# Residual scaling x + alpha·fx: a contiguous head for the first 30.5 KiB of each partition

## The chip, the cores and the metric

The kernel runs on one core of a Trainium2 chip. The metric is the device time of one execution in microseconds. All numbers of the profile come from one profiled execution; where nothing else is said, a time is counted from the start of that execution's span.

## The reference

The inputs `x` and `fx` have the shape 512 x 32 x 640 in bf16, 20.97 MB each, and `alpha` holds one bf16 number. The output has the shape of `x`:

```python
def reference(x, fx, alpha):
    return x + alpha * fx
```

Each byte of `x` and `fx` is read once, each byte of the output is written once: 62.9 MB in all.

## The kernel before

Each tensor is taken as one long row of numbers and cut into 128 equal parts, one for each partition: partition p owns the 160 KiB from p times 160 KiB on. The code counts in units of `K = 512` numbers, which is 1 KiB a partition in bf16 (128 KiB over all partitions), so that a partition's part has `ROW = 160` units. One tile `t` of 160 + 47.5 units holds everything. x lies at its own units 0 to 160, and the result is written over it. fx is put wherever the tile is free at that time, first over the later units of x that have not been loaded yet, then in the units 160 to 207.5.

The order of all work is written out by hand in `PLAN`, one step a line, and is the order in which the instructions stand on their engines:

- `x a b` loads units a to b of x (`load_x`, L96), `f a b p` loads units a to b of fx to place p of the tile (`load_f`, L100). Both are DMAs issued by SyncE (SP).
- `a` loads alpha (L104), spreads it over the partitions with one small matmul (L108) and copies it to `a_f` (L110).
- `m a b` multiplies units a to b of fx in place by alpha (L113), `c a b` adds them to x (L116). Both run on VectorE (DVE).
- `s a b` stores units a to b (L119), again from SP. A step behind a `|` names another step that this one has to wait for: the first store waits for the multiply of units 112.5 to 134.5.

Waits follow from the places in the tile. `x 95 160` writes over the place of fx 0 to 65 and so waits for the add over those units; `f 112.5 142.5 160` and `f 142.5 160 190` write over the place of fx 65 to 112.5 and wait for its adds. All DMAs are issued by SP in the order of the plan, on one queue (q1), so that a DMA whose wait is not over holds back those behind it. Each runs on 16 DMA engines, 8 partitions on each; each engine carries the same bytes. A row of a partition that is longer than 64 KiB is moved as two packets, any other as one. At the end SP waits for all but the last store (L131), and the program ends when the last store has landed.

The partition's part is named here:

```python
xv, fv, ov = (
    t.flatten_outer_dims().rearrange("(p n) d -> p (n d)", p=P) for t in (x, fx, out)
)
```

and `of(v, a, b)` (L87) cuts units a to b out of it, for loads and stores alike.

Of the kernel before, what the change touches and what calls it, by code (L numbers as in the profile page):

```python
# [1 line left out]

# [4 lines left out]

ALU = mybir.AluOpType
F32 = mybir.dt.float32

P = 128
K = 512
ROW = 160
SPARE = 47.5

LANES = 8

PLAN = """
f 0 8 95
a
f 8 65 103  # L30
x 0 64
x 64 95
f 65 112.5 160
m 0 8
m 8 65
c 0 8
c 8 64
c 64 65
x 95 160
m 65 95  # L40
c 65 95
f 112.5 142.5 160
m 95 112.5
c 95 112.5
f 142.5 160 190
m 112.5 134.5
s 0 64 | m 112.5 134.5
m 134.5 142.5
c 112.5 142.5
m 142.5 160  # L50
c 142.5 160
s 64 128
s 128 160
"""


@with_exitstack
def kernel(
    ctx: ExitStack,
    tc: tile.TileContext,  # L60
    x: bass.AP,
    fx: bass.AP,
    alpha: bass.AP,
    out: bass.AP,
):
    nc = tc.nc
    xv, fv, ov = (
        t.flatten_outer_dims().rearrange("(p n) d -> p (n d)", p=P) for t in (x, fx, out)
    )
    assert xv.shape[1] == ROW * K  # L70

    consts = ctx.enter_context(tc.tile_pool(name="consts", bufs=1))
    psum = ctx.enter_context(tc.tile_pool(name="psum", bufs=1, space=bass.MemoryType.PSUM))
    flat = ctx.enter_context(tc.tile_pool(name="flat", bufs=1))
    ctx.enter_context(tc.manual_schedule())
    t = flat.tile([P, int((ROW + SPARE) * K)], x.dtype, name="t")
    info = mybir.DependencyInfo(mybir.DependencyClass.Sync, mybir.DependencyReason.DATA)

    lanes = {}
    lies = []  # L80
    done = []

    def at(a, b):
        return t[:, int(a * K) : int(b * K)]

    def of(v, a, b):
        return v[:, int(a * K) : int(b * K)]  # L87

    def place(a, b):
        for c, d, p in reversed(lies):  # L90
            if c <= a and b <= d:
                return at(p + a - c, p + b - c)
        raise ValueError(f"fx {a} to {b} lies nowhere in one piece")

    def load_x(a, b):
        done.append(nc.sync.dma_start(out=at(a, b), in_=of(xv, a, b)))  # L96

    def load_f(a, b, p):
        lies.append((a, b, p))
        done.append(nc.sync.dma_start(out=at(p, p + b - a), in_=of(fv, a, b)))  # L100

    def load_alpha():
        a_n = consts.tile([LANES, 1], alpha.dtype, name="a_n")
        done.append(nc.sync.dma_start(out=a_n[:], in_=alpha[None, :].to_broadcast([LANES, 1])))  # L104
        ones = consts.tile([1, P], alpha.dtype, name="ones")
        nc.vector.memset(ones[:], 1.0)  # L106
        a_ps = psum.tile([P, 1], F32, name="a_ps")
        done.append(nc.tensor.matmul(a_ps[:], ones[:], a_n[0:1, :], start=True, stop=True))  # L108
        lanes["a"] = consts.tile([P, 1], F32, name="a_f")
        nc.vector.tensor_copy(out=lanes["a"][:], in_=a_ps[:])  # L110

    def multiply(a, b):
        done.append(nc.vector.tensor_scalar_mul(place(a, b), place(a, b), lanes["a"][:]))  # L113

    def add(a, b):
        done.append(nc.vector.tensor_add(at(a, b), at(a, b), place(a, b)))  # L116

    def store(a, b):
        done.append(nc.sync.dma_start(out=of(ov, a, b), in_=at(a, b)))  # L119

    does = {"x": load_x, "f": load_f, "a": load_alpha, "m": multiply, "c": add, "s": store}
    begun = {}
    for step in filter(None, PLAN.split("\n")):
        step, *later = step.split(" | ")
        what, *numbers = step.split()
        does[what](*map(float, numbers))
        begun[step] = done[-1]
        for other in later:
            tc.add_manual_dep(done[-1].ins, begun[other].ins.name, info, reason="begins late")

    rest = nc.sync.nop(nofuse=True)  # L131
    for i in done[:-1]:
        tc.add_manual_dep(rest.ins, i.ins.name, info, reason="all but the last store")


# [1 line left out]
_INS = ['x', 'fx', 'alpha']  # L137
_OUTS = [((512, 32, 640), 'bfloat16')]


# [23 lines left out]
```

## Time and profile before

| | before |
|---|---|
| median of the runs | 151.1 us (3 runs, 151.07 to 151.1) |
| the profiled execution's own time | 151.11 us |
| its span | 149.3 us |
| DMA packets, bytes | 1728, 62.92 MB |
| HBM read, written | 41.94 MB, 20.97 MB |
| DVE busy | 66.5 us in 16 instructions |

The span lies inside the profiled execution's own time; 1.8 us are outside of it. The granted clock was 1.0 throughout. A packet is the piece of one partition's row that a DMA engine moves at a time; the trace has its start, its length and its bytes, but not its engine. 192 of the 1728 packets are smaller than 512 B: alpha's and those that count up semaphores.

### The profile page before, as it was taken

The numbers are of one execution on the slowest core, as the hardware profiler recorded it, in microseconds if no ns is written. First come the engines' busy times: TensorE is split into PE (matmuls) and PEld (weight loads), VectorE is DVE, ScalarE is ACT, GpSimd is POOL, SyncE is SP. The second block draws the span as 40 slices with busy tenths as digits, with TensorE's granted clock in tenths as the row PEclk, the third lists the DMA queues.
The fourth block names the chain that finished last, engine by engine and source line by source line (L and its number), as shares of the span: only waits on it lengthen the run. The fifth ranks groups of instructions, "written<-read, shape, count | busy, mean of one in ns | idle before, by whom it ended". The sixth has DMA issues, their size and how long they took to land.

```text
span 149.3 us, 84 instructions
## 1 busy us (share of the span) xinstructions
PE 0.2 (0%) x1; PEld 0.1 (0%) x1; DVE 66.5 (45%) x16; POOL 0.2 (0%) x4
## 2 busy tenths in 40 slices
PE   0000000000000000000000000000000000000000
PEld 0000000000000000000000000000000000000000
DVE  0300008920069999029997093599997000000000
POOL 0000000000000000000000000000000000000000
DMA  5969998969699999999999999899896969697993
GB/s 147 603 281 500 500 461 351 562 281 562 281 408 451 438 417 443 456 429 428 428 428 428 417 444 469 378 526 492 351 562 281 562 281 562 281 562 307 456 474 167
DMA packets 1728, 62.92 MB, mean 421 GB/s; under 512 B 192, under 2 KB 192, under 8 KB 192
## 3 DMA queue, kind: packets, MB, share of 16 engines
q1 hardware_dynamic: 1728, 62.92, 98.0%
HBM read 41.94 MB, written 20.97 MB: 421 GB/s over the span
## 4 chain that ended last, share of the span: by engine, by line
DMA 38%; DVE 33%; another core or an unknown queue 4%; SPq 1%; issue 0%; DVEq 0%
DMA t<-in_x_dram 27%; DVE t L116 26%; DMA t<-in_fx_dram 11%; DVE t L113 7%; SPq L100 0%; SPq L104 0%; DVEq L116 0%
## 5 line engine op out<-in xcount | busy, mean ns | idle before, releaser
L116 DVE TENSOR_TENSOR t<-t 128x15360 bf16<-128x15360 bf16 (+4 forms) x7 | 43.6, 6252 | 16.6 <-DMA t<-in_x_dram 16.5
L113 DVE TENSOR_SCALAR t<-t,a_f 128x4096 bf16<-128x4096 bf16 (+4 forms) x7 | 22.8, 3265 | 25.7 <-DMA t<-in_fx_dram 25.7
L110 DVE COPY a_f<-a_ps 128x1 f32<-128x1 f32 x1 | 0.2, 159 | 5.2 <-PE a_ps L108 5.2
L106 DVE MEMSET ones<- 1x128 bf16 x1 | 0.2, 165 | 0.8 <-PEq L148 0.8
L108 PE MATMUL a_ps<-a_n,ones 1*128 1x1 bf16 x1 | 0.2, 158 | 6.0 <-DMA a_n<-in_alpha_dram 6.0
L148 POOL MEMSET const-bfloat16-1.0<- 128x1 bf16 x1 | 0.1, 102 | 0.0
L148 POOL MEMSET const-uint8-127<- 128x1 uint8 x1 | 0.1, 102 | 0.0
L148 POOL MEMSET const-float32-1.0<- 128x1 f32 x1 | 0.1, 99 | 0.0
L108 PEld LDWEIGHTS <-ones 1*128 1x128 bf16 x1 | 0.1, 98 | 1.0 <-DVE ones L106 1.0
L148 POOL MEMSET const-float32-0.0<- 128x1 f32 x1 | 0.1, 98 | 0.2 <-issue 0.2
## 6 DMA issues: line engine op xcount, KB each, us to landing
t<-in_x_dram SPq DMA_DIRECT2D x1, 8320.0 KB, 25.8
t<-in_fx_dram SPq DMA_DIRECT2D x1, 7296.0 KB, 21.4
t<-in_fx_dram SPq DMA_DIRECT2D x1, 6080.0 KB, 63.0
out_dram<-t SPq DMA_DIRECT2D x1, 4096.0 KB, 33.7
t<-in_x_dram SPq DMA_DIRECT2D x1, 3968.0 KB, 49.3
t<-in_fx_dram SPq DMA_DIRECT2D x1, 3840.0 KB, 16.4
t<-in_fx_dram SPq DMA_DIRECT2D x1, 2240.0 KB, 9.5
t<-in_fx_dram SPq DMA_DIRECT2D x1, 1024.0 KB, 5.0
```

The lines of the kernel that those rows point to most:

```text
L106: nc.vector.memset(ones[:], 1.0)
L108: done.append(nc.tensor.matmul(a_ps[:], ones[:], a_n[0:1, :], start=True, stop=True))
L110: nc.vector.tensor_copy(out=lanes["a"][:], in_=a_ps[:])
L113: done.append(nc.vector.tensor_scalar_mul(place(a, b), place(a, b), lanes["a"][:]))
L116: done.append(nc.vector.tensor_add(at(a, b), at(a, b), place(a, b)))
L148: nc = _bacc.Bacc("TRN2", target_bir_lowering=False, num_devices=1)
```

## The change

The tensors are no longer cut into 128 equal parts. The first 128 x 30.5 KiB of each tensor are a head, cut into 128 parts of 30.5 KiB that lie end to end in memory; the rest is a body, cut into 128 parts of 129.5 KiB. Partition p owns part p of the head (units 0 to 30.5) and part p of the body (units 30.5 to 160). The operation is elementwise, so any such cut gives the same output as long as x, fx and the output are cut alike. The distance between the rows of neighbouring partitions in memory thus goes from 160 KiB to 30.5 KiB in the head and to 129.5 KiB in the body.

The plan is cut anew along the head's border, since no transfer may cross it. The first load is fx 0 to 30.5 in place of fx 0 to 8, and the second is fx 30.5 to 65 in place of 8 to 65. x 30.5 to 94.5 is loaded ahead of x 0 to 30.5, and the adds stand in that order too; two adds over units 0 to 65 take the place of three. There are eight loads of x and fx and three stores, as before. The stores were of 64, 64 and 32 units; they are of 30.5, 64 and 65.5 units.

```diff
+HEAD = 30.5
...
 PLAN = """
-f 0 8 95
+f 0 30.5 95
 a
-f 8 65 103
-x 0 64
-x 64 95
+f 30.5 65 125.5
+x 30.5 94.5
+x 0 30.5
 f 65 112.5 160
-m 0 8
-m 8 65
-c 0 8
-c 8 64
-c 64 65
-x 95 160
-m 65 95
-c 65 95
-f 112.5 142.5 160
-m 95 112.5
-c 95 112.5
-f 142.5 160 190
+m 0 30.5
+m 30.5 65
+c 30.5 65
+c 0 30.5
+x 94.5 160
+m 65 94.5
+c 65 94.5
+f 112.5 142 160
+m 94.5 112.5
+c 94.5 112.5
+f 142 160 189.5
 m 112.5 134.5
-s 0 64 | m 112.5 134.5
-m 134.5 142.5
-c 112.5 142.5
-m 142.5 160
-c 142.5 160
-s 64 128
-s 128 160
+s 0 30.5 | m 112.5 134.5
+m 134.5 142
+c 112.5 142
+m 142 160
+c 142 160
+s 30.5 94.5
+s 94.5 160
 """
...
-    xv, fv, ov = (
-        t.flatten_outer_dims().rearrange("(p n) d -> p (n d)", p=P) for t in (x, fx, out)
-    )
-    assert xv.shape[1] == ROW * K
+    xv, fv, ov = (t.flatten_outer_dims().rearrange("n d -> (n d)") for t in (x, fx, out))
+    assert xv.shape[0] == P * ROW * K
...
     def of(v, a, b):
-        return v[:, int(a * K) : int(b * K)]
+        assert b <= HEAD or a >= HEAD
+        at_head = b <= HEAD
+        part = v[: int(P * HEAD * K)] if at_head else v[int(P * HEAD * K) :]
+        shift = 0 if at_head else HEAD
+        return part.rearrange("(p n) -> p n", p=P)[:, int((a - shift) * K) : int((b - shift) * K)]
```

## The prediction

> **What bounds the kernel now.** I read the page's slices first (section 2), then its DMA sums (section 3), then a table of busy time by stretch, then SP's instructions in order of time, and last the trace's single DMA packets (start, length, size).
>
> The page, its slices and its queue sums:
>
> ```profile
> span 149.3 us, 84 instructions
> ...
> DVE  0300008920069999029997093599997000000000
> ...
> DMA  5969998969699999999999999899896969697993
> ...
> q1 hardware_dynamic: 1728, 62.92, 98.0%
> HBM read 41.94 MB, written 20.97 MB: 421 GB/s over the span
> ```
>
> The 16 DMA engines work for 98.0% of the span, VectorE (DVE) for 45%. The alternation of 9 and 6 in the DMA row comes from packets counted whole in one slice. From the single packets I counted how many run in each microsecond: 16 of 16 from 3.1 us after the span's start to about 147. So there is no gap to close in the middle, and the chain of waits (section 4 of the page, which names 33% DVE) misleads here: those DVE steps sit beside a full DMA queue.
>
> The busy table of the first microseconds (columns: stretch, its length, busy time by engine, clock, DMA share, GB/s):
>
> ```profile
> 1.75:2.75 1.00, 0.00 (x0) 0.00 (x0) 0.00 (x0) 0.00 (x0) 1.00 0.96 188
> 2.75:3.75 1.00, 0.00 (x0) 0.00 (x0) 0.00 (x0) 0.00 (x0) 1.00 0.93 352
> 3.75:4.75 1.00, 0.00 (x0) 0.00 (x0) 0.00 (x0) 0.00 (x0) 1.00 0.97 410
> ...
> 10.00:50.00 40.00, 0.00 (x0) 0.00 (x0) 15.41 (x3) 0.00 (x0) 1.00 0.98 426
> ...
> 99.00:147.00 48.00, 0.00 (x0) 0.00 (x0) 15.77 (x4) 0.00 (x0) 1.00 1.01 438
> ```
>
> The engines are busy from the first packet on, but move 188 and then 352 GB/s before they reach the 426 to 438 of loads and stores. Steady packets fit one line within 0.4 ns: 36.77 ps a byte and 7.7 ns a packet (8192 B in 0.309 us, 65536 B in 2.418). By it one engine's share, 3,932,160 B in 96 packets, takes 145.34 us. The rest of the 149.3 is 1.75 before the first packet, the slow start, some 0.2 of packets over the line, and 1.2 behind the last packet (148.16).
>
> The slow start is the one place with time in it. The first packets seen took 0.69 to 1.44 us instead of 0.309. An engine has 8 packets in the first load: 8 x 0.309 = 2.47, so the second load could begin at 1.75 + 2.47 = 4.22. Its first packets start at 4.80 on the fastest engine, 5.09 on the mean and 5.40 on the slowest: losses of 0.58, 0.87 and 1.18. Every engine then carries equal bytes, so the lag stays: at the end the semaphores of the 16 engines arrive from 148.12 to 148.59. The slowest sets the time.
>
> **The change part by part.**
>
> *DVE.* From the rows by shape, an add costs (15,086 - 8,157) / (28,672 - 15,360) = 0.5205 ns an element, a multiply (7,820 - 4,220) / (29,184 - 15,360) = 0.2604. One small add goes (0.42 us) and sizes shift. All of it lies beside DMA, so its price is zero as long as no load or store is issued too late. SP's rows:
>
> ```profile
> 0.73 0.38 SPq L100 DMA_DIRECT2D t<-in_fx_dram  x1
> ...
> 60.07 0.38 SPq L96 DMA_DIRECT2D t<-in_x_dram  x1
> 78.58 12.53 SPq L100 DMA_DIRECT2D t<-in_fx_dram  x2
> 98.15 17.05 SPq L119 DMA_DIRECT2D out_dram<-t  x3
> ```
>
> The first issue, at 0.73, has its first packet at 1.75: 1.02 us. Each later issue must come that long before the first engine runs dry.
> - x 94.5-160 waits for both adds over fx 0 to 65. x 30.5-94.5 ends at 129 units of 1 KiB a partition, as x 0-64 does now, so the adds begin at 42.41: 9.36 (17,664 elements) + 8.29 (15,616) end at 60.1, where today's end at 60.04. The second add needs x 0-30.5, due at about 51.6, when the first ends at 51.8; a wait of some tenths is covered. The first engine runs dry at 65.09: 4.0 spare. SP waits here with the two fx loads queued behind it, as today.
> - f 112.5-142 follows 4.15 of multiply and 8.02 of add from 66.14: 78.4, with 84.8 the dry point, 5.4 spare.
> - f 142-160: x 94.5-160 lands after 272.5 units as now (85.9), add 4.96, issue 90.9; the load before it is half a unit shorter, so the dry point moves from 93.90 to 93.75: 1.8 spare.
> - s 0-30.5 waits for m 112.5-134.5, which starts 0.15 earlier: issue at 98.0 instead of 98.15, dry point 99.35, so 0.3 spare instead of 0.2. This is the thinnest cover; uncovered, each 0.1 us late costs 0.1.
> - s 30.5-94.5 then needs only an add done near 78 and finished loads, so it is issued at once (the second store waits until 107.54 now). The last store waits for c 142-160, done near 114.8; 94.5 units of stores, 28.6 us, cover it until 128.
> - alpha stands in the queue behind 30.5 units instead of 8 and lands near 13 instead of 6. The first multiplies then run near 13 (4.3 us) and 23 (4.8); their adds begin at 42.4. Free.
>
> *Packets.* A partition's part of the stores goes from three packets to four (rows over 64 KiB are cut in two): 128 more, 8 an engine, 8 x 7.7 ns = +0.06 us, all on the bound. Bytes and the twelve DMAs stay.
>
> *Row starts.* Packets whose row starts off a whole KiB in memory lie above the line: in the median by 2.3 to 2.6 ns (17920, 30720 and half of the 33280 B), in the mean by up to 9.7. That the start is the cause is a reading, not shown. Now 24 of an engine's 96 packets start so; with pitches of 30.5 and 129.5 KiB it is 60 of 104. 36 x 2.4 ns = +0.09; ends: 0 if it is not the start, and 36 x 7.4 = +0.27 with all of today's excess (0.18 us an engine over 24 packets). I take 0.09, the median.
>
> *The first load.* In place of 8 KiB rows 160 KiB apart, the engines start on 30.5 KiB rows lying end to end. The trace shows no other cold start, so I bound it. Nothing gained: the slowest still loses 1.18. All gained: only what the quickest first packet lost, 0.694 - 0.309 = 0.39, stays, a gain of 0.79. I take the slowest at today's mean, 1.18 - 0.87 = 0.31, because part of the spread looks like queueing: 14 first packets end one after another from 2.57 to 3.19 us, some 47 ns apart, and rows at other distances may collide less. [...]
>
> *Sum.* -0.31 + 0.06 + 0.09 = -0.16. The profiled execution took 151.11 us, 1.8 beyond its span, and the median is 151.1: 150.95.
>
> **Rivals.**
> - *The slow start goes wholly* (a collision of evenly spaced rows). For: the 188 and 352 GB/s with all engines busy, and a packet that started 0.6 us behind the others took only 0.307. Against: no row shows another spacing at a cold start. 151.1 - 0.79 + 0.15 = 150.45.
> - *The contiguous head does nothing*: the start is latency, equal for any address. For: even the quickest first packet lost 0.39, and first touches of x at 22 us, mid-stream, cost nothing at the same pitch. Only the two costs stay: 151.25. The Trainium skill says as much, "Perfetto Trace Analysis", section "Contiguity and DMAs": contiguity matters only within a partition's line. By that rule the head buys nothing; only the steady rows agree.
> - *Slower: the uneven pitch costs every row.* For: the two fx loads all of whose rows start at half KiBs have means 4.2 and 9.7 ns above the line. If 104 packets an engine paid 9.7 ns, that is 1.0 us, less the 0.2 paid now, plus 0.06: with nothing gained at the start 151.95, with 0.31 gained 151.65. It decides against the change from about 6 ns a packet (0.6 over 104). Against: the medians show 2.4, and the 48,640 B rows at an odd KiB pay nothing.
>
> **How the numbers follow.** The forecast has 0.40, the start gone 0.32, the head doing nothing 0.13, the costly pitch 0.15. A measurement of this kernel can tell about 0.2%, 0.3 us, from no change. Faster by more: all of the second and 0.05 of the first, 0.37. Slower by more: the last and 0.02 of the third, 0.17. Within: 0.46. The likeliest case, 150.95, has 150.75 to 151.2 as its own range; to hold 8 in 10 the range reaches to 150.4 (the start gone, nearly whole) and 151.4 (a part of the row costs).
>
> **What would show it.** In the profile after: DMA busy share again about 98%; GB/s in the first three microseconds above 188, 352 and 410 and a narrower spread of the last store's 16 semaphores (0.47 us now) if the start gained; packets of 64 KiB still 2.418 us, or some ns more if the pitch costs; 1856 packets on q1; SP's issues near 60.1, 78.4, 90.9, 98.0. The forecast is wrong if DMA shows a hole near 99 us (the first store came late), or if steady packets of equal size changed their length.

## The result and the profile after

The change makes the kernel slower: 151.34 us in the median of 22 runs, against 151.10 in 22 runs of the kernel before, a ratio of 1.0020 with a 95% interval from 1.0014 to 1.0025. In the experiments below the changed kernel was measured again on three other occasions, beside the kernel before on the same chip: 1.0052 (1.0039 to 1.0066), 1.0044 (1.0028 to 1.0060) and 1.0030 (1.0019 to 1.0041). The forecast was 150.95, a gain of 0.15 us. The measured time lies inside the range that went with it (150.4 to 151.4), but on the slower side of no change.

The profiled execution took 151.47 us. Its page, with the lines that answer to those of the prediction (span; busy tenths of VectorE and of the DMA engines in 40 slices; the queue's packets, megabytes and busy share):

```profile
span 149.7 us, 83 instructions
...
DVE  0005608400069999039995093699996000000000
...
DMA  6999997969699899979999999999998998999993
...
q1 hardware_dynamic: 1856, 62.92, 97.9%
HBM read 41.94 MB, written 20.97 MB: 420 GB/s over the span
```

The queue has the 128 packets more that were counted out, its busy share is the same, and the span is 0.4 us longer. SP's rows in order of time (start, length, what):

```profile
60.06 0.38 SPq L100 DMA_DIRECT2D t<-in_x_dram  x1
78.28 13.03 SPq L104 DMA_DIRECT2D t<-in_fx_dram  x2
98.06 17.10 SPq L123 DMA_DIRECT2D out_dram<-t  x3
```

Every issue stands within 0.12 us of where the prediction put it. So the plan on SP and VectorE runs as worked out, and the time went where these rows don't show it: into single packets. I followed the semaphores by which each of the 16 DMA engines reports a landing; the slowest engine's, and the distance to the engines' mean where it matters:

| | before | after | difference |
|---|---|---|---|
| 129 units landed (the first 64-unit load of x) | 42.32 | 42.38 | +0.06 |
| 272.5 units landed (x up to 160) | 85.84 | 85.90 | +0.06 |
| all 320 units landed, slowest engine | 100.29 | 100.59 | +0.30 |
| all landed, mean of the engines | 100.04 | 100.06 | +0.02 |
| last store landed, slowest engine | 148.59 | 148.93 | +0.34 |
| last store landed, mean of the engines | 148.34 | 148.41 | +0.07 |

The mean engine is 0.07 us later, about what the 8 more packets were to cost (0.06). The rest, 0.27 us, is one engine that falls behind the others in the last load of fx, between 85.9 and 100.6 us. It is there in the packets: of the 16 engines' first packets of that load (18,432 B, 0.688 us in the median), four took 1.42, 0.84, 0.79 and 0.78 us. In the kernel before two were late (1.16 and 0.98 instead of 0.669). The trace doesn't name their engines, but the slowest engine was 0.30 us behind the mean before that load and 0.25 us after it, so they must have fallen on engines that were ahead, where they cost nothing.

What leads to that load, from the timeline of both kernels, 85 to 96 us (first the kernel before, then the changed one; in brackets the idle time in front and what ended it):

```profile
85.94 4.83 DVE L116 TENSOR_TENSOR t<-t 128x8960 bf16<-128x8960 bf16 x1 [4.91 <-DMA t<-in_x_dram]
90.79 0.33 SPq L100 DMA_DIRECT2D t<-in_fx_dram  x1
94.97 3.15 DVE L113 TENSOR_SCALAR t<-t,a_f 128x11264 bf16<-128x11264 bf16 x1 [4.21 <-DMA t<-in_fx_dram]
```

```profile
85.99 4.96 DVE L120 TENSOR_TENSOR t<-t 128x9216 bf16<-128x9216 bf16 x1 [5.21 <-DMA t<-in_x_dram]
90.98 0.33 SPq L104 DMA_DIRECT2D t<-in_fx_dram  x1
94.88 3.15 DVE L117 TENSOR_SCALAR t<-t,a_f 128x11264 bf16<-128x11264 bf16 x1 [3.93 <-DMA t<-in_fx_dram]
```

The add that frees the place of the last load is half a unit longer (4.96 against 4.83) and the load ahead of it half a unit shorter. The first engine reaches the last load at 93.90 before and 93.82 after, so the lead, from issue to the first engine's need, went from 3.11 to 2.84 us. The prediction held 1.02 us to be enough.

The other place of the change, the cold start (stretch, length, busy times, clock, DMA share, GB/s):

```profile
1.75:2.75 1.00, 0.00 (x0) 0.00 (x0) 0.00 (x0) 0.00 (x0) 1.00 1.63 437
2.75:3.75 1.00, 0.00 (x0) 0.00 (x0) 0.00 (x0) 0.00 (x0) 1.00 0.67 281
3.75:4.75 1.00, 0.00 (x0) 0.00 (x0) 0.00 (x0) 0.00 (x0) 1.00 0.66 281
```

These rows must not be read as a faster start: packets are counted whole where they begin, and 31,232 B packets begin almost four times less often. The packets themselves lost 0.75 us an engine over the steady line in the start, against 0.69 before. This start did not gain.

### The profile page after: what moved, and what is told of

Same layout as the page of the kernel before. It is cut to its first block, busy times and chain, and to the rows that moved or that the text cites. A ratio compares the mean times of both kernels' runs of the same rounds, so it can differ in the third digit from the quotient of the medians.

```text
span 149.7 us, 83 instructions
## 1 busy us (share of the span) xinstructions
PE 0.2 (0%) x1; PEld 0.1 (0%) x1; DVE 66.5 (44%) x15; POOL 0.2 (0%) x4
## 3 DMA queue, kind: packets, MB, share of 16 engines
q1 hardware_dynamic: 1856, 62.92, 97.9%
## 4 chain that ended last, share of the span: by engine, by line
DMA 38%; DVE 33%; another core or an unknown queue 4%; SPq 1%; issue 0%; DVEq 0%
DMA t<-in_x_dram 27%; DVE t L120 26%; DMA t<-in_fx_dram 11%; DVE t L117 7%; SPq L104 0%; SPq L108 0%; DVEq L120 0%
## 5 line engine op out<-in xcount | busy, mean ns | idle before, releaser
L120 DVE TENSOR_TENSOR t<-t 128x15104 bf16<-128x15104 bf16 (+3 forms) x6 | 43.5, 7269 | 19.9 <-DMA t<-in_x_dram 19.8
L117 DVE TENSOR_SCALAR t<-t,a_f 128x9216 bf16<-128x9216 bf16 (+5 forms) x7 | 22.8, 3265 | 15.7 <-DMA t<-in_fx_dram 15.7
```

## The experiments

The theory after the result was **short lead**: the last load is issued too late for its first packets, and the slowest engine of the 16 sets the end. Its rivals were the layout (contiguous head, distance of rows), the stores, and the last load's own geometry. The comparisons of one group share a chip and the runs of the kernel before, whose median stands at the group's head; each result is the median time, its ratio to the kernel before and the ratio's 95% interval. The lead is the time from the issue of the last load to its first packet; "late" is a packet of the last load over 0.05 us above the steady line of 36.77 ps a byte and 7.7 ns a packet. The profiled execution of each kernel is one sample, and the share of late packets differs from execution to execution.

**First group: what of the plan or the layout.** The kernel before stood at 150.91 us. The changed kernel itself was not among these four; the late store (e4), which gained nothing, stands in for it.

Early load (e1):

```diff
-x 94.5 160
+x 94.5 112.5
+x 112.5 160
```

> The changed kernel with x 94.5-160 loaded in two DMAs (94.5-112.5, then 112.5-160), so that the add over units 94.5-112.5 ends near 83 instead of 91 and the last load of fx can be issued some 7.5 us earlier, 10 us before the engines run dry instead of 2.84. Theory 'short lead': the extra 0.73, 0.16, 0.10 and 0.10 us of four of that load's first packets are the price of the short lead; they vanish (no packet over 0.05 us above the line near 94 us) and the time falls by 0.2 to 0.4 us to about 151.0. Rival 'place': the fourth wait, the tile's last units or the count of descriptors makes these packets slow whenever the load starts; they stay, and the time stays at 151.3. Rival 'pitch': the loss lies in all rows; 151.3 too.

Measured: 151.25 us, 1.0015 (1.0005 to 1.0025). The load is issued at 85.64, 8.16 us ahead, and has no late packet; its slowest engine is 0.22 us behind the mean after it, as before the change (0.25). The time is above the 151.0 that 'short lead' expected.

Late load (e2; eight memsets of a small tile, 0.13 us each, behind the add):

```diff
+w 8
-f 142 160 189.5
+f 142 160 189.5 | w 8
...
```

> The changed kernel with eight tiny memsets on VectorE behind the add over 94.5-112.5, and the last load of fx held until they are done: issued about 1 us later, some 1.8 us before the engines run dry. Theory 'short lead': more and longer late packets at the start of that load, the slowest engine later by up to 1 us; time 151.5 to 152.3. Rivals 'place' and 'pitch': the load is still in time by the 1.02 us that the cold start took from issue to first packet; 151.3, the same few late packets.

Measured: 153.37 us, 1.0164 (1.0131 to 1.0196). The timeline:

```profile
86.02 4.96 DVE L121 TENSOR_TENSOR t<-t 128x9216 bf16<-128x9216 bf16 x1 [5.20 <-DMA t<-in_x_dram]
90.93 1.00 DVE L129 MEMSET idle<- 128x8 f32 x8
91.96 0.33 SPq L105 DMA_DIRECT2D t<-in_fx_dram  x1
```

An issue 0.98 us later, still 1.96 us ahead of the first engine's need, costs some 2 us (1.9 over the late store, e4). 36 of the load's 128 packets are late, by 14.4 us in all, up to 101 us and so far behind the first ones; between 94 and 95 us 11.7 packets run at a time on the mean instead of 16. The slowest engine lands at 103.27, 2.16 behind the mean. The price is larger than any theory had said, above 'short lead' too (151.5 to 152.3).

Old parts (e3; the changed plan on the kernel before's equal parts of 160 KiB):

```diff
-    xv, fv, ov = (t.flatten_outer_dims().rearrange("n d -> (n d)") for t in (x, fx, out))
+    xv, fv, ov = (t.flatten_outer_dims().rearrange("(p n) d -> p (n d)", p=P) for t in (x, fx, out))
...
+        return v[:, int(a * K) : int(b * K)]
```

> The changed kernel's plan on the 160 KiB equal parts of the kernel before: no contiguous head, all else as in the changed kernel. Rival 'pitch' (contiguous head and 129.5 KiB rows cost): back to 151.1, less the 0.06 us of 128 more packets, so 151.15. Theory 'short lead' (the plan costs, the layout does nothing): 151.3, like the changed kernel, with the cold start unchanged (the slowest engine 1.2 us behind).

Measured: 151.69 us, 1.0038 (1.0022 to 1.0053): with no contiguous head the plan costs as much, nine late packets at a lead of 2.75 us. That is more than either theory had said. The start lost 0.71 us an engine, within what kernels with the head lost (0.56 to 0.75).

Late store (e4):

```diff
-s 30.5 94.5
+s 30.5 94.5 | c 112.5 142
```

> The changed kernel with its second store held until the add over 112.5-142 is done, near 107 us as in the kernel before, instead of being issued at 98.5 while the last load still runs. Rival 'two stores at the turn': the descriptors of two stores disturb the last load and the first store; time falls to 151.1. Theory 'short lead': 151.3, nothing moves, since the late packets lie near 94 us, 4 us ahead of the stores' issue.

Measured: 151.48 us, 1.0038 (1.0022 to 1.0053). Holding the second store until 107 us gains nothing; the late packets near 94 us stay (two, the worst by 0.70 us). With this kernel as the measure on this chip, the early load took off 0.23 us, although it adds a DMA.

**Second group: single parts on the kernel before** (150.94 us).

> The changed kernel as it is, beside the next three on one chip, as their measure. Expected 151.3 to 151.5 (1.002 to 1.004 of the kernel before), with one to six late packets at the start of the last load near 94 us.

Measured: 151.70 us, 1.0052 (1.0039 to 1.0066), slower than expected; seven late packets at a lead of 2.82 us, slowest engine 1.06 behind the mean after the last load.

Early load in the kernel before (e6):

```diff
-x 95 160
+x 95 112.5
+x 112.5 160
```

> The kernel before with x 95-160 loaded in two DMAs (95-112.5, then 112.5-160), so that the last load of fx is issued near 86 instead of 90.8. Theory 'short lead': no late packets near 94 us; since its own lead of 3.11 us cost little (two late packets on engines that were ahead), the time falls by 0 to 0.2 us, 150.9 to 151.1. Rival 'place': the two late packets stay, no gain.

Measured: 151.16 us, 1.0011 (0.9997 to 1.0024). No late packet, no gain either: the kernel before loses nothing that can be measured to its own lead, or the added DMA takes it back.

Kernel before, later load (e7; two memsets, 0.27 us):

```diff
+w 2
-f 142.5 160 190
+f 142.5 160 190 | w 2
...
```

> The kernel before with two tiny memsets behind the add over 95-112.5 and the last load of fx held for them: 0.27 us less lead, 2.84 us, what the changed kernel has, with the old layout, plan, packets and stores. Theory 'short lead': most of the changed kernel's loss comes back, +0.15 to +0.3 us over the kernel before, with a few more late packets near 94 us. Rivals (packets, layout, stores): +0.0.

Measured: 150.96 us, 1.0008 (0.9995 to 1.0021), two late packets. No clear loss: the 0.15 to 0.3 us of 'short lead' did not come. The run also did not reach the lead that it was made for: its engines stood close together after the start, so that x landed early on the slowest and the lead was 3.18 us, not 2.84.

Stores alone (e8):

```diff
-s 0 64 | m 112.5 134.5
+s 0 30.5 | m 112.5 134.5
...
-s 64 128
-s 128 160
+s 30.5 94.5
+s 94.5 160
```

> The kernel before with the changed kernel's stores alone: 30.5, 64 and 65.5 units in place of 64, 64 and 32, the second issued at once behind the first, a fourth packet for each partition. Rival 'packets and stores': +0.06 us for 8 more packets an engine at 7.7 ns, and up to +0.25 if the early second store costs. Theory 'short lead': +0.06 alone.

Measured: 151.04 us, 1.0010 (0.9996 to 1.0023): no clear loss. The 0.06 us of packets would fit, and the interval leaves room for more.

**Third group: the same lead by other cuts** (151.03 us).

Head of 31 KiB (e9; x cut at 95 and fx at 142.5, as before the change):

```diff
-HEAD = 30.5
+HEAD = 31
...
-c 94.5 112.5
-f 142 160 189.5
+c 95 112.5
+f 142.5 160 190
...
```

> A contiguous head of 31 KiB instead of 30.5, so that x is cut at 95 and fx at 142.5, as in the kernel before: the add ahead of the last load is 17.5 units instead of 18 and the load in front of it 30 instead of 29.5. Everything else (head, order of loads, stores, packets, number of DMAs) as in the changed kernel. Theory 'short lead': the lead grows by 0.27 us to 3.1 or more, the late packets near 94 us drop to two or none, and the time goes from the changed kernel's 151.4 to 151.7 down to about 151.1 (1.000 to 1.0015 of the kernel before). Rival 'layout and stores': like the changed kernel, 1.003 to 1.005.

Measured: 151.77 us, 1.0048 (1.0034 to 1.0063). The expectation fails on the time, and the lead did not come back (2.59 us). The last load has no late packet, but the start spread the engines wider: near 65 us, at the landing of fx 65-112.5, the slowest was at 66.58, 1.08 behind the fastest (0.35 to 0.67 in the kernels without this head). A slow engine lets x land late, so the add and each issue behind it come late. The first store was late too: issued at 98.63 instead of 98.06, 0.85 us ahead of its first packet, with 11.9 packets running in the quarter of a microsecond after 99.25. That is where this kernel's mean engine lost time (it ends at 148.56, against 148.41 in the changed kernel), so its loss lies in the start and the first store, not in late packets of the last load. The lead is spent by the spread of the engines as well as by the plan.

Kernel before, much later load (e10; five memsets, 0.67 us):

```diff
+w 5
-f 142.5 160 190
+f 142.5 160 190 | w 5
...
```

> The kernel before with five tiny memsets behind the add over 95-112.5 and the last load held for them: 0.67 us less lead, some 2.5 us, with the old layout, plan and stores. Theory 'short lead': between the changed kernel at 2.8 (1.002 to 1.005) and the run with a lead of 1.96 (1.016): six or more late packets, 1.004 to 1.009. Rivals (layout, packets, stores): 1.000.

Measured: 151.30 us, 1.0018 (1.0003 to 1.0033). A loss, as 'short lead' has it, but less than half of what was expected at a lead of 2.74 us; its profiled execution (150.89, with one late packet) was the fastest of twelve, from 150.89 to 151.87.

Head of 31 KiB with two memsets (e11):

```diff
+w 2
-f 142.5 160 190
+f 142.5 160 190 | w 2
...
```

> The kernel with the 31 KiB head and two tiny memsets ahead of the last load: its lead cut by 0.27 us, to that of the changed kernel. Theory 'short lead': the loss of the changed kernel comes back, 1.002 to 1.005, with late packets near 94 us. Rival 'the odd cuts of the 30.5 KiB head cost' (rows off a whole KiB): stays as the run without the memsets.

Measured: 151.93 us, 1.0072 (1.0051 to 1.0093); 0.16 us over the same kernel without the memsets, with a lead of 2.23 us and three late packets. The loss is larger than both expectations. Here too the engines were spread, by 1.34 us near 65 us, and the first store came late (issued at 98.93, 0.84 us ahead of its first packet; 6.9 packets running in the quarter after 99.5), so the two causes are mixed in it.

> The changed kernel once more, as the measure of the other three on their chip: 1.002 to 1.005 of the kernel before, late packets near 94 us, the more of them the wider the engines are spread after the cold start.

Measured: 151.59 us, 1.0044 (1.0028 to 1.0060); eight late packets at a lead of 2.72 us.

**Fourth group: each suspect by itself** (150.91 us).

Shorter add (e13):

```diff
-c 94.5 112.5
+c 94.5 108.5
```

> The changed kernel with its add over units 94.5-112.5 cut to 94.5-108.5 (units 108.5-112.5 of the output lack alpha fx): the last load of fx is issued 1.07 us earlier, some 3.9 us ahead, with no DMA added and no size, place or address of any transfer changed. Theory 'short lead': no late packet at the start of the last load, and 0.3 us or more less than the changed kernel on the same chip, 1.000 to 1.002 of the kernel before. Rival 'geometry of the last load' (18 KiB rows at place 189.5): late packets stay, 1.003 to 1.005.

The timeline:

```profile
85.97 3.89 DVE L120 TENSOR_TENSOR t<-t 128x7168 bf16<-128x7168 bf16 x1 [5.21 <-DMA t<-in_x_dram]
89.89 0.33 SPq L104 DMA_DIRECT2D t<-in_fx_dram  x1
```

Measured: 151.15 us, 1.0011 (0.9998 to 1.0024), against 151.35 for the changed kernel beside it. The lead of 3.92 us leaves no late packet. No transfer has another size, place or address; only the moment of issue moved, and 0.20 us of the loss of 0.44 went, less than the 0.3 expected. (The output lacks alpha fx in four units; no transfer depends on that.)

Cut at 142 in the kernel before (e14):

```diff
-f 112.5 142.5 160
+f 112.5 142 160
...
-f 142.5 160 190
+f 142 160 189.5
...
```

> The kernel before with fx cut at 142 instead of 142.5, so that its last load has the changed kernel's 18 KiB rows at place 189.5 behind one of 29.5 KiB rows, and nothing else of the change. Its lead is shorter by the 0.15 us of half a unit, 2.9 to 3.1 us. Rival 'geometry': four or more late packets, 1.002 to 1.004. Theory 'short lead' alone: two or three late packets, 1.000 to 1.001.

Measured: 151.03 us, 1.0008 (0.9995 to 1.0021), two late packets of 0.18 and 0.15 us at a lead of 3.28. The geometry of the last load shows no clear cost by itself at this lead; at a lead under 3 us it was not tried on the old plan.

First load alone (e15):

```diff
-f 0 8 95
+f 0 30.5 95
 a
-f 8 65 103
+f 30.5 65 125.5
...
```

> The kernel before with its first load of 30.5 units instead of 8 (multiplies and adds cut to match), on the old equal parts: the other loads, all stores and the last load as before. Theory 'cold start': after a first load in long rows the engines stay further apart (slowest engine 0.1 to 0.2 us later at 42 us), so 1.0005 to 1.0015, and the lead of the last load shrinks with the spread. Rival 'the first load is free': 1.000.

Measured: 151.25 us, 1.0020 (1.0007 to 1.0032). Of the parts tried alone on the kernel before it is the only one whose interval leaves out 1. In its profiled execution the slowest engine landed x 0-64 at 42.31, against 42.00 in the kernel with the cut at 142 beside it, and three packets of the last load were late at a lead of 3.11.

> The changed kernel once more, as the measure of the other three on their chip: 1.002 to 1.005.

Measured: 151.35 us, 1.0030 (1.0019 to 1.0041). Its profiled execution, 151.11, was the fastest of twelve; it has three late packets at a lead of 2.92 us.

**Last group: taking both out of the changed kernel** (150.86 us).

Small first load (e17):

```diff
-f 0 30.5 95
+f 0 8 95
 a
+f 8 30.5 103
...
```

> The changed kernel with its first load cut in two, fx 0-8 and fx 8-30.5, both from the contiguous head: the first rows are 8 KiB again, 30.5 KiB apart, and there is one DMA and one packet a partition more. Theory 'long first rows': the slowest engine is back by 0.1 to 0.2 us at 42 us, the engines stand closer together, the lead of the last load grows by as much, and the time falls by 0.15 to 0.3 us from the changed kernel's 151.35 to 151.6: 1.001 to 1.002 of the kernel before, although a DMA and 0.06 us of packets are added. Rival 'the first load plays no part': no better than the changed kernel, 1.003 or more.

Measured: 151.46 us, 1.0049 (1.0035 to 1.0063), five runs from 151.01 to 151.85. The expectation fails: 8 KiB rows at the start did not help the changed kernel. Their first effect did come: the slowest engine landed 129 units at 42.19 us (42.27 to 42.39 in the four profiled executions of the changed kernel). But the profiled execution was the 151.01 one, with two late packets at a lead of 2.97 us, so that the loss of the other four is in no trace.

Small first load and early load (e18):

```diff
-x 94.5 160
+x 94.5 112.5
+x 112.5 160
...
```

> The same with x 94.5-160 loaded in two DMAs, so that the last load is issued near 86: both causes taken away in the changed kernel. If long first rows and the short lead are the whole of it, what is left is the price of 16 more packets an engine and two more DMAs, 1.0005 to 1.0015 of the kernel before. If it stays at 1.003, a cause is missing.

Measured: 151.10 us, 1.0016 (1.0007 to 1.0025): 0.36 us less than the same kernel with the load issued late, and no late packet at a lead of 8.20.

No version tried beats the kernel before.

## Why the prediction was wrong

**What bounds the kernel: right.** DMA's share is 97.9%, 16 packets run at a time from 3 us to about 147, steady packets kept their length (65,536 B in 2.418 us), and no order of VectorE's work shows in the time except through an issue.

**VectorE and SP: right in the times, wrong in what they are worth.** The adds came at 9.36 and 8.28 us (forecast 9.36 and 8.29), the issues at 60.06, 78.28, 90.98 and 98.06 (60.1, 78.4, 90.9, 98.0). The first step that failed is the sentence that each issue must come "that long", 1.02 us, before the first engine runs dry. That figure was taken from the one cold issue, where nothing was queued and where the first packets were themselves late by up to 1.1 us. For the first store, the issue that the prediction feared for, it held: issued 1.26 us ahead of its first packet in the changed kernel, it had no late packet and 16 packets kept running; at 0.85 us ahead the engines ran short (e9). For the last load it did not hold, although "1.8 spare" was right as a time:

| the last load's rows | lead in us: late packets, one execution each |
|---|---|
| 18 KiB, the changed plan | 8.20: 0, 8.16: 0, 3.92: 0, 2.97: 2, 2.93: 2, 2.92: 3, 2.84: 4, 2.82: 7, 2.75: 9, 2.72: 8, 1.96: 36 |
| 18 KiB, the plan before (e14) | 3.28: 2 |
| 17.5 KiB | 8.01: 0, 3.30: 0, 3.18: 2, 3.11: 2 and 3, 2.74: 1, 2.59: 0, 2.23: 3 |

On the changed plan the late packets grow as the lead shrinks; with 17.5 KiB rows much less so. The cleanest pair that differs in the moment of issue is the shorter add against the changed kernel (0.20 us of a loss of 0.44); the early load against the late store (0.23 of 0.57) and the two kernels with the small first load (0.36 of 0.60) agree, with a DMA added. So a load issued at least 1 us earlier gives back about half of the loss, where the prediction's price was nothing. That the 0.27 us which the new cuts took from the lead made that half is not shown: on the plan before, 0.67 us less cost 0.27 us (e10), and an attempt at 0.27 us less (e7) lost nothing clear.

**Packets and row starts: small, as forecast.** 0.06 + 0.09 were forecast; the mean engine ended 0.07 later, half of that. The rows off a whole KiB are not told apart from the packets by this.

**The first load: wrong in sign.** This is the second step that failed, and in the sum the larger one. A gain of 0.31, with bounds of 0 and 0.79, was built on reading the queue of first packets as colliding rows. In the two profiled executions the slowest engine landed the first 129 units 0.06 later, not 0.31 earlier. The start lost 0.56 to 0.75 us an engine in eight executions of kernels with the 30.5 KiB head and first load, and 0.69 and 0.71 in the two with the same 30.5 KiB rows 160 KiB apart (e15, e3): the distance of rows shows no effect there, as the rival "the contiguous head does nothing" had it. That rival's 151.25 lacked a price for the longer first load: on the old layout that load, with the multiplies and adds cut to match, made the time 1.0020 of the kernel before (e15). A loss should have been among the bounds, since nothing in the trace excluded one. How that loss comes about is only partly seen: over six profiled executions of kernels with an 8 KiB start on the old layout the slowest engine landed the first 129 units at 42.0 to 42.4, over ten with a 30.5 KiB start at 42.2 to 42.4, means 42.15 and 42.32; what the slowest engine loses there also comes off the lead of the last load.

**The sum.** Forecast were -0.31 + 0.06 + 0.09 = -0.16 us; measured are +0.24. In the profiled pair the slowest engine was 0.06 us later after the first load of x and still at 85.9, 0.30 later after the last load of fx, for which the sum had no term, and 0.34 at the end. That the time stayed inside the range is luck: the range reached up to 151.4 for a cost of the rows that did not come.

**The layout.** What the Trainium skill says in "Perfetto Trace Analysis", section "Contiguity and DMAs" (contiguity matters only within a partition's line), agrees with the runs: undoing the head left 1.0038, where the changed kernel with only its second store held back had 1.0038.

**The rival on the slower side** (every row pays for the new pitch) did not happen; steady packets stayed within 3.2 ns of the line in the median. The 9.7 ns a packet that this rival took from the last load was no price of a row start: two late packets, of 0.49 and 0.32 us, make 6.3 ns of that mean, and without them it is 3.5. So the late packets stood in the trace before, and were read as rows that cost more. Slower came in part from a wait that the prediction had declared covered.

**What stays open.** With the lead given back, the kernels are still 0.1 to 0.2% slower than the kernel before (1.0015, 1.0011, 1.0016), of which 8 packets an engine are 0.06 us; the remainder was not told apart from the first load's part. The three parts tried alone on the kernel before (stores 1.0010, cut at 142 1.0008, first load 1.0020) add up to 0.38%, about what the whole change cost, but each is uncertain by 0.13%; the new order of x's loads was never tried alone. At nearly the same lead the kernel before lost less (1.0018 at 2.74 us) than the changed one (1.0044 at 2.72). The cut alone doesn't explain it at a lead of 3.28 us; whether 18 KiB rows need a longer lead than 17.5 KiB rows was not tried. Why a small first load helped nothing in the changed kernel isn't settled, and neither is what makes a load late that was issued 2.8 us ahead: no record here shows what happens between the issue and a packet's start.

## What to carry to other kernels

On a queue that is always full, ask of every transfer that waits for something how long before the engines' need it is issued, and take the price of a short lead from a transfer of the same kind in the middle of the stream, not from a cold start: here one microsecond more of lead for one load was worth 0.2 us, three times the price of 8 more packets an engine. Look at a load's single packets before averaging them: two late ones can pass for a small cost of every row. The end is set by the slowest of the DMA engines, so compare the spread of the 16 landings, not only their mean. Half a unit shifted between two pieces, done to make borders fit, moves both ends of such a lead.

## What the runs showed of the hardware

- A load issued 1.96 us ahead of the first engine's need left engines idle (11.7 of 16 packets running between 94 and 95 us) and made 36 of 128 packets late, almost to its end; a store issued 1.26 us ahead of the first engine's need, in the changed kernel, had no late packet. The cold start's first packet came 1.02 us after its issue.
- The delay of a late packet stays with its engine: in the changed kernel's profile the slowest engine was 0.54 us behind the mean after the last load and 0.52 after the last store, 48 us later.
- With a head of 31 KiB instead of 30.5 the start spread the engines by 1.08 and 1.34 us near 65 us, in both kernels that had it, against 0.35 to 0.67 in all others. Both the row's length and the distance of rows changed there, and no run tells them apart.
